# One-token attention over a long cache: value loads issued on ScalarE's queue instead of SyncE's

## The chip, the cores and the metric

The kernel runs on one core of a Trainium2 chip. The metric is the device time of one execution in microseconds (us); the value of the kernel before is the median of two runs. The profile is one execution of the same program, recorded by the hardware profiler; its times are counted from the first instruction of the span.

## The reference

One transformer block for a single token (sequence length 1, width 640) with conditioning. What matters for the time is the attention: 32 heads, each with its own keys and values of 16384 x 128 in bf16.

```python
mod = (_silu(c) @ w_mod)                   # six vectors of 640: sa, ca, ga, sb, cb, gb
h = _layernorm(x) * (1 + ca) + sa
q = h @ wq                                 # 32 heads of 128
scores = einsum('bhqd,bhkd->bhqk', q, k_cache) * 128 ** -0.5
p = softmax(scores)
o = einsum('bhqk,bhkd->bhqd', p, v_cache)
x = x + ga * (o @ wo)
h = _layernorm(x) * (1 + cb) + sb
x = x + gb * ((silu(h @ w_gate) * (h @ w_up)) @ w_down)
```

The keys of a head are 4 MiB (4096 KB in the profile's lists) and so are its values: 256 MiB over 32 heads. All weights together are 22 MB more. Nothing is used twice, so everything goes once from HBM into SBUF.

## The kernel before

**An order written out by hand.** The program is built by a small planner (`_Plan`). Every operation is given an engine, a position (a number that looks like a time in us), the operations that it depends on, and a function that emits it. `emit` sorts the operations of each engine by position; each engine then runs its list strictly in that order, and waits on a semaphore ahead of an operation where a dependency is not already known to be met. A position therefore decides only the order on its engine. `plan.dma` adds a transfer; its engine is `"sp"` (SyncE) unless `eng` says otherwise, and a transfer waits in the list of the engine that issues it like any other operation. All transfers are recorded at L71.

**Heads.** `TK(h)` is 20.0 + 19.8 h, the nominal start of head h. For each head:

- VectorE (DVE) multiplies the keys by the query in place (L420, one instruction over 128 x 16384), adds halves in three folds (L422, L429 twice), reduces to 128 x 128 scores (L432, `o_red[h]`) and takes the maximum of each partition (L435).
- GpSimd (POOL) makes the maximum over partitions (L438); ScalarE (ACT) turns it into a bias (L440) and writes the exponentials (L442, `o_exp[h]`); POOL sums (L445); ACT inverts the sum by logarithm and exponential (L447, L449).
- TensorE (PE) multiplies the exponentials by the values in 32 matmuls (L459, `o_pvlast[h]`). ACT scales the result into SBUF (L465, "acc"), PE folds it (L472), and ACT places it for the output product (L493, L496, or L505 for the last four heads).

**Rings.** `kring` has two slots for keys and `vring`, inside the tile `vbig`, two for values; head h uses slot h % 2. The keys of head h+1 may be loaded once `o_red[h-1]` has read the slot for the last time; the values of head h once `o_pvlast[h-2]` has. The query weights lie over a part of `vring`, so the first two value loads wait for all query products (`o_q_all`). Each load of a head is 128 rows, one per partition, of 32 KB contiguous in HBM. The keys of head 0 come in four parts and the values of head 31 in three (`VSPLIT`).

**Queues before.** SyncE's list is: the conditioning weights, the query weights, the keys of heads 0 and 1, then values 0, keys 2, values 1, keys 3, values 2 and so on, with keys h+1 directly ahead of values h. After keys 31 and values 30 come the output weights `wo` in three transfers (position `TL + 9.0`), the three parts of values 31, and, once `o_red[31]` is done, the feed-forward weights (`w_gate`, `w_up`, and `w_down` in five transfers), which lie over the key slots. ACT issues only the two tiny loads of `c` and `x` at the start.

**End.** After the values of head 31 have been multiplied (L483) come the output product (L541), a layer norm, gate and up (L605), down (L623), a transpose and the store.

Of the kernel before, what the change touches and what calls it, by code (L numbers as in the profile page):

```python
# [141 lines left out]
def build(nc, A_x, A_k, A_v, A_wq, A_wo, B_wg, B_wu, B_wd, c_in, w_mod, out):  # L142
    H, S, Dh = A_k.shape[1], A_k.shape[2], A_k.shape[3]
# [19 lines left out]
    def TK(h):  # L163
        return 20.0 + PERIOD * h

    es = ExitStack()
    with es:
        block = es.enter_context(nc.Block())
        plan = _Plan(nc, es)
# [15 lines left out]
        vring = vbig[:, 0:2 * TT * 128].rearrange("p (s t d) -> p s t d", s=2, t=TT)  # L185
# [126 lines left out]
        def f_mod(e, wv, m0, m1, cols):  # L312
# [11 lines left out]
            deps=[o_mod, o_xn], name="t1")  # L324
# [36 lines left out]
        kv = lambda t, h: t[0, h].rearrange("(p t) d -> p t d", p=128)  # L361
        d_k = [None] * H
        d_v = [None] * H
# [10 lines left out]
        def load_k(h):  # L374
            s2 = h % 2
            deps = [o_red[h - 2]] if h >= 2 else []
            if h == 0:
                KP = TT // NKP0
                d_k[0] = [plan.dma(0.2 + 0.01 * c, kring[:, 0, c * KP:(c + 1) * KP, :], kv(A_k, 0)[:, c * KP:(c + 1) * KP, :],
                                   ("k0", c), name="dma_k0_%d" % c) for c in range(NKP0)]  # L380
                return
            d_k[h] = [plan.dma(TK(h - 1) + 8.8 if h > 1 else 0.3, kring[:, s2], kv(A_k, h), ("k", s2), deps=deps, name="dma_k%d" % h)]

        def load_v(h, pos):
            s2 = h % 2
            cuts = VSPLIT if h == H - 1 else [0, TT]
            deps = [o_pvlast[h - 2]] if h >= 2 else o_q_all
            d_v[h] = [plan.dma(pos + 0.01 * c, vring[:, s2, a:b, :], kv(A_v, h)[:, a:b, :],
                               ("v", s2, c), deps=deps, name="dma_v%d_%d" % (h, c)) for c, (a, b) in enumerate(zip(cuts, cuts[1:]))]

        load_k(0)
        load_k(1)
# [13 lines left out]
        for h in range(H):  # L406
            base = TK(h)
            s2 = h % 2
            if h + 1 < H and h >= 1:
                load_k(h + 1)  # L410
            load_v(h, base + 8.9 + (0.5 if h == H - 1 else 0.0))

            kslot = kring[:, s2]
            npc = len(d_k[h])
# [2 lines left out]
            for c in range(npc):  # L417
# [3 lines left out]
                         deps=[d_k[h][c], o_qbc[h]], name="mult%d_%d" % (h, c))  # L421
                fd.append(op(DVE, base + 3.3 * c + 2.2 + (6.6 if npc == 1 else 0.0), lambda e, ksl=ksl: e.tensor_tensor(  # L422
                    out=ksl[:, :, 0:64], in0=ksl[:, :, 0:64], in1=ksl[:, :, 64:128], op=ALU.add),
                    deps=[o_m], name="fold1_%d_%d" % (h, c)))
            prev = fd
            w = 64
            for i in range(2):
# [3 lines left out]
                    deps=prev, name="fold%d_%d" % (i + 2, h))]  # L431
            o_red[h] = op(DVE, base + 18.2, lambda e, s2=s2, kslot=kslot, w=w: e.tensor_reduce(  # L432
                out=S_sb[:, s2], in_=kslot[:, :, 0:w], axis=AX.X, op=ALU.add),
                deps=prev + [o_exp[h - 2] if h >= 2 else None], name="red%d" % h)
# [9 lines left out]
                deps=[o_nb, o_red[h], o_pvlast[h - 2] if h >= 2 else None], name="exp%d" % h)  # L444
# [8 lines left out]
            if h < H - 1:  # L453


                def f_pv(e, s2=s2):
# [10 lines left out]
                    deps=[o_pvlast[h], o_rl, o_diag[h - 2] if h >= 2 else None], name="acc%d" % h)  # L467
# [21 lines left out]
            if h < HD:  # L489
# [5 lines left out]
                    deps=[done, o_rl], name="on%d" % h)  # L495
                o_z[h] = op(ACT, base + 29.2, lambda e, h=h, g=g, n=n, o=(h - h0) * jw, jw=jw: e.activation(  # L496
                    out=Z[:, g, o:o + jw], in_=msk[n][:], func=ACTF.Copy, scale=on_f[:, h:h + 1]),
                    deps=[o_on[h], o_msk[n]], name="z%d" % h)
                if h == h0 + n - 1:
                    o_am = op(PE, base + 29.4, lambda e, g=g, n=n: e.matmul(A_ps[:, 0:n], lhsT=Z[:, g], rhs=e8[n][:], start=True, stop=True),  # L500
                              deps=[o_z[i] for i in range(h0, h0 + n)] + [o_e8[n], o_as[g - 1] if g else None], name="am%d" % g)
                    o_as[g] = op(ACT, base + 29.6, lambda e, h0=h0, n=n: e.activation(out=A_sb[:, h0:h0 + n], in_=A_ps[:, 0:n], func=ACTF.Copy),
                                 deps=[o_am], name="as%d" % g)
            else:
                o_on[h] = op(ACT, base + 29.0 + (0.7 if h == H - 1 else 0.0), lambda e, h=h, sc=sc: e.activation(  # L505
                    out=On[:, h - HD:h - HD + 1], in_=OT_ps[:, h:h + 1], func=ACTF.Copy, scale=sc),
                    deps=[done, o_rl], name="on%d" % h)
# [4 lines left out]
        a = 0  # L512
        while a < len(GROUPS):
            b = a
            while b < len(GROUPS) and GROUPS[b][1] == GROUPS[a][1]:
                b += 1
            (h0, n), h1 = GROUPS[a], GROUPS[b - 1][0] + GROUPS[b - 1][1]
            d = plan.dma(TO + 0.01 * a, wo_v[:, h0:h1, :].rearrange("p (g k) n -> p g (k n)", k=n),
                         A_wo[h0 * 128:h1 * 128, :].rearrange("(g p k) n -> p g (k n)", p=128, k=n),
                         ("wo", a), deps=[o_mod_b, o_mod], name="dma_wo%d" % a)  # L520
            d_wo += [d] * (b - a)
            a = b
# [4 lines left out]
        for g in list(range(len(GROUPS))) + [None] * (H - HD):  # L527
            if g is not None:
                ks = [k for k, gg in wo_seq if gg == g]
                deps, pos = [o_as[g], d_wo[g]], TL + 29.45 + 0.005 * g  # L530
            else:
                k = HD + len(o_wo) - len(GROUPS)
                ks = [k]
                deps, pos = [o_on[k], d_wo1], TL + (29.48 + 0.001 * (k - HD) if k < H - 1 else 29.8)
# [39 lines left out]
        for a in range(2 * NP2, FCH):  # L574
# [6 lines left out]
                  deps=[o_abf, o_modc], name="ga_attn")  # L581
        o_x1 = op(DVE, TE + 0.2, lambda e: e.scalar_tensor_tensor(
            out=x1[:], in0=tt2[:], scalar=1.0, in1=x_res[:], op0=ALU.mult, op1=ALU.add, accum_out=st[:, 4:5]),
            deps=[o_ga, o_xf], name="x1")
# [3 lines left out]
            deps=[o_xc1, o_rstd1, o_onep_b], name="t2")  # L588
        o_h2 = op(DVE, TE + 1.1, lambda e: e.tensor_tensor(out=h2_col[:], in0=tt3[:], in1=sb_, op=ALU.add),
                  deps=[o_t2], name="h2_col")  # L590
# [26 lines left out]
        for i, (a, b) in enumerate(wd_parts):  # L617
            def f_down(e, a=a, b=b):
                last = None
                for cc in range(KC):  # L620
# [7 lines left out]
                  deps=[prev, o_modc], name="gb_ffn")  # L628
# [10 lines left out]
def bass_adaLN_cond__gqa_block_cached__swiglu_ffn__decode_kernel(  # L639
    nc: bass.Bass,  # L640
    A_x: bass.AP,
    A_k_cache: bass.AP,
    A_v_cache: bass.AP,
    A_wq: bass.AP,
    A_wo: bass.AP,
    B_x: bass.AP,
    B_w_gate: bass.AP,
    B_w_up: bass.AP,
    B_w_down: bass.AP,
    c: bass.AP,  # L650
    w_mod: bass.AP,
    out: bass.AP,
):
    build(nc, A_x, A_k_cache, A_v_cache, A_wq, A_wo, B_w_gate, B_w_up, B_w_down, c, w_mod, out)
# [28 lines left out]
```

## Time and profile before

| | |
|---|---|
| time, median of 2 runs | 689.57 us (689.49 to 689.65) |
| span of the profiled execution | 684.5 us, 4723 instructions |
| the rest of a run's time, outside the span | 5.05 us (689.57 less 684.5) |
| VectorE busy | 617.5 us, 90% of the span |
| TensorE, ScalarE, GpSimd busy | 351.0, 79.6 and 360.0 us |
| moved by DMA | 290.79 MB, mean 425 GB/s |
| share of the transfers' packets on SyncE's queue (q1) | 13668 packets, 290.48 MB |
| on ScalarE's queue (q10) | 288 packets, under 0.01 MB |

The profile gives its execution no time other than its span, so sums are made against the 684.5 us, and 5.05 us are added to come to the time of a run. Busy time is not the measure here: two resources, VectorE and the 16 DMA engines, are both close to full over nearly the whole span, and the question is which of them waits for the other, and when.

### The profile page before, as it was taken

What the parts mean: (1) busy time and instruction counts of PE and PEld (TensorE: products, weight loads), DVE (VectorE), ACT (ScalarE), POOL (GpSimd) and SP (SyncE); (2) the same over time, 40 slices, a digit from 0 to 9 for tenths busy, and PEclk for the clock granted to TensorE, in tenths of its full rate; (3) what the DMA queues carried; (4) which work ended last, traced back from release to release, by engine and by line L of the source; (5) the groups of instructions that cost most, each with busy time, mean ns of one, the idle gap of its engine ahead of it and who ended that gap; (6) DMA issues with size and microseconds to landing.
All of it is one profiled execution on the core that took longest, in us unless ns stands there. A gap on an engine that the chain in (4) does not pass through costs nothing.

```text
span 684.5 us, 4723 instructions
## 1 busy us (share of the span) xinstructions
PE 351.0 (51%) x1941; PEld 150.8 (22%) x1942; DVE 617.5 (90%) x226; ACT 79.6 (12%) x281; POOL 360.0 (53%) x71
## 2 busy tenths in 40 slices
PE   0545344656554454655554444565544545655464
PEld 0322111222221121222221121222211212222154
DVE  0299999999999999999999999999999999999911
ACT  0111011011101111011101111011101110111010
POOL 0005765655567765655567766655533644555400
PEclk9976677676677667677777767767776677677765
DMA  8999999999999999999999999999999999999997
GB/s 369 417 438 432 431 429 437 429 433 433 429 434 431 431 429 430 433 431 434 433 431 429 433 429 431 430 431 433 432 433 433 429 432 429 435 433 428 413 413 277
DMA packets 13979, 290.79 MB, mean 425 GB/s; under 512 B 1605, under 2 KB 2309, under 8 KB 4485
## 3 DMA queue, kind: packets, MB, share of 16 engines
q1 hardware_dynamic: 13668, 290.48, 99.1%
q8 instruction: 15, 0.25, 0.1%
q10 hardware_dynamic: 288, 0.00, 0.0%
q14 instruction: 8, 0.06, 0.0%
HBM read 290.48 MB, written 0.00 MB: 424 GB/s over the span
## 4 chain that ended last, share of the span: by engine, by line
DVE 79%; DMA 18%; SPq 2%; issue 1%; PE 0%; ACT 0%; DVEq 0%
DVE kring L420 35%; DVE kring L422 18%; DVE kring L429 14%; DMA kring<-in_A_k_cache_dram 12%; DVE S_sb L432 9%; DMA vbig<-in_A_wq_dram 4%; SPq L71 2%; DMA kring<-in_B_w_down_dram 2%; DVE pm L435 1%; PE psb L339 0%; PE psb L623 0%; ACT qbc L343 0%; DVE e L402 0%; DVE msk L397 0%; PE psb L631 0%
## 5 line engine op out<-in xcount | busy, mean ns | idle before, releaser
L459 PE MATMUL psb<-vbig,P_sb 128*4 128x512 bf16 x992 | 284.4, 458 | 268.1 <-ACT P_sb L442 193.9
L438 POOL PARTITION_ALL_REDUCE gm<-pm x32 | 229.2, 7163 | 239.9 <-DVE pm L435 239.9
L420 DVE TENSOR_TENSOR kring<-kring,qbc 128x16384 bf16<-128x16384 bf16 (+1 forms) x35 | 278.4, 7953 | 5.9 <-ACT qbc L343 4.6
L459 PEld LDWEIGHTS psb<-vbig,P_sb 128*4 128x4 bf16 x992 | 94.8, 98 | 444.6 <-ACT P_sb L442 219.9
L445 POOL PARTITION_ALL_REDUCE Ls<-rs x32 | 129.7, 4054 | 34.2 <-ACT P_sb L442 34.2
L422 DVE TENSOR_TENSOR kring<-kring 128x8192 bf16<-128x8192 bf16 (+1 forms) x35 | 142.1, 4059 | 1.2
L429 DVE TENSOR_TENSOR kring<-kring 128x4096 bf16<-128x4096 bf16 x64 | 112.5, 1758 | 2.2
L432 DVE TENSOR_REDUCE S_sb<-kring 128x128 f32<-128x2048 bf16 x32 | 73.2, 2286 | 1.1
L472 PE MATMUL psb<-ident_f,acc_sb 4*128 4x1 f32 x248 | 32.5, 248 | 23.8 <-ACT acc_sb L465 23.8
L465 ACT ACTIVATE acc_sb<-psb,rl 4x512 f32<-4x512 f32 x31 | 21.0, 677 | 176.2 <-PE psb L459 176.2
L472 PEld LDWEIGHTS psb<-ident_f,acc_sb 4*128 4x128 f32 x248 | 29.8, 186 | 39.5 <-ACT acc_sb L465 39.5
L440 ACT ACTIVATE nb<-gm 128x1 f32<-128x1 f32 x32 | 6.4, 201 | 193.6 <-POOL gm L438 193.6
L447 ACT ACTIVATE lnl<-Ls 128x1 f32<-128x1 f32 x32 | 6.5, 203 | 133.7 <-POOL Ls L445 133.7
L580 DVE TENSOR_TENSOR tt<-attn_bf,modb 128x5 f32<-128x5 bf16 x1 | 0.2, 166 | 14.5 <-ACT attn_bf L579 14.5
L442 ACT ACTIVATE P_sb<-S_sb,nb 128x128 bf16<-128x128 f32 x32 | 12.9, 402 | 1.2
L289 PE MATMUL psb<-st,ones_f 128*128 128x1 f32 x4 | 1.2, 363 | 22.8 <-ACT x_f L306 22.1
L339 PE MATMUL psb<-vbig,h_col 128*128 128x512 bf16 x39 | 10.8, 448 | 2.4 <-DMA vbig<-in_A_wq_dram 2.4
L291 DVE SCALAR_TENSOR_TENSOR xc<-x_f,psb 128x5 f32<-128x5 f32 x1 | 0.2, 161 | 12.2 <-PE psb L289 12.2
L435 DVE TENSOR_REDUCE pm<-S_sb 128x1 f32<-128x128 f32 x32 | 9.2, 286 | 1.1
L496 ACT ACTIVATE Z<-msk,on_f 128x16 bf16<-128x16 f32 (+1 forms) x28 | 8.7, 310 | 0.9
L493 ACT ACTIVATE on_f<-psb 128x1 f32<-128x1 f32 x28 | 4.8, 171 | 31.9 <-PE psb L472 30.7
L283 DVE TENSOR_SCALAR dd<-ec 128x5 f32<-128x5 f32 x1 | 0.2, 172 | 8.9 <-ACT ec L282 8.9
(72 smaller groups left out, 78.3 us busy)
## 6 DMA issues: line engine op xcount, KB each, us to landing
kring<-in_A_k_cache_dram SPq DMA_DIRECT2D x31, 4096.0 KB, 18.4
vbig<-in_A_v_cache_dram SPq DMA_DIRECT2D x31, 4096.0 KB, 27.6
vbig<-in_A_wq_dram SPq DMA_DIRECT2D x1, 5120.0 KB, 26.5
wreg<-in_w_mod_dram SPq DMA_DIRECT2D x1, 4800.0 KB, 14.6
kring<-in_A_k_cache_dram SPq DMA_DIRECT2D x4, 1024.0 KB, 31.4
wreg<-in_A_wo_dram SPq DMA_DIRECT2D x1, 3840.0 KB, 38.0
kring<-in_B_w_gate_dram SPq DMA_DIRECT2D x1, 2160.0 KB, 18.9
kring<-in_B_w_up_dram SPq DMA_DIRECT2D x1, 2160.0 KB, 23.8
```

What stands on the lines that cost most here:

```text
L71: return e.dma_start(out_ap, in_ap)
L420: o_m = op(DVE, base + 3.3 * c, lambda e, ksl=ksl, qb=qb: e.tensor_tensor(out=ksl, in0=ksl, in1=qb, op=ALU.mult), deps=[d_k[h][c], o_qbc[h ...
L422: fd.append(op(DVE, base + 3.3 * c + 2.2 + (6.6 if npc == 1 else 0.0), lambda e, ksl=ksl: e.tensor_tensor(out=ksl[:, :, 0:64], in0=ksl[:, ...
L429: prev = [op(DVE, base + 15.5 + 1.5 * i, lambda e, kslot=kslot, w=w: e.tensor_tensor(out=kslot[:, :, 0:w], in0=kslot[:, :, 0:w], in1=kslot ...
L432: o_red[h] = op(DVE, base + 18.2, lambda e, s2=s2, kslot=kslot, w=w: e.tensor_reduce(out=S_sb[:, s2], in_=kslot[:, :, 0:w], axis=AX.X, op= ...
L435: o_max = op(DVE, base + 18.5, lambda e, h=h, s2=s2: e.tensor_reduce(out=pm[:, h:h + 1], in_=S_sb[:, s2], axis=AX.X, op=ALU.max), deps=[o_ ...
L438: o_gm = op(POOL, base + 19.0, lambda e, h=h: e.partition_all_reduce(gm[:, h:h + 1], pm[:, h:h + 1], channels=128, reduce_op=bass.bass_isa ...
L442: o_exp[h] = op(ACT, base + 19.4, lambda e, h=h, s2=s2: e.activation(out=P_sb[:, s2], in_=S_sb[:, s2], func=ACTF.Exp, scale=SCALE, bias=nb ...
L445: o_L = op(POOL, base + 20.0, lambda e, h=h: e.partition_all_reduce(Ls[:, h:h + 1], rs[:, h:h + 1], channels=128, reduce_op=bass.bass_isa. ...
L459: last = e.matmul(acc_ps[s2][0:4, :], lhsT=P_sb[:, s2, 4 * c:4 * c + 4], rhs=vring[:, s2, 4 * c:4 * c + 4, :].rearrange("p t d -> p (t d)" ...
L465: o_acc[h] = op(ACT, base + 28.6, lambda e, h=h, s2=s2: e.activation(out=acc_sb[:, s2], in_=acc_ps[s2][0:4, :], func=ACTF.Copy, scale=rl[0 ...
L472: last = e.matmul(OT_ps[:, h:h + 1], lhsT=acc_sb[:, s2, 128 * i:128 * (i + 1)], rhs=ident_f[:, i:i + 1], start=(i == 0), stop=(i == 3))
```

## The change

The values are issued from ScalarE's list (`eng="act"`), and their position moves from 8.9 after the start of head h to 28.65 after the start of head h-2. That is the place right behind the scaling at L465 ("acc", 28.6) of head h-2, ahead of that head's L493 and L496 and of L440 of head h-1. Values 0 and 1 stand at 4.75 and 4.85, behind the last copies of the query stage on ACT (L356, L394). The dependencies are as before. Keys and all weights stay on SyncE, in the same order, without the values between them.

```diff
@@ load_v(h, pos)
             s2 = h % 2
             cuts = VSPLIT if h == H - 1 else [0, TT]
             deps = [o_pvlast[h - 2]] if h >= 2 else o_q_all
-            d_v[h] = [plan.dma(pos + 0.01 * c, vring[:, s2, a:b, :], kv(A_v, h)[:, a:b, :],
-                               ("v", s2, c), deps=deps, name="dma_v%d_%d" % (h, c)) for c, (a, b) in enumerate(zip(cuts, cuts[1:]))]
+            d_v[h] = [plan.dma(pos + 0.01 * c, vring[:, s2, a:b, :], kv(A_v, h)[:, a:b, :], ("v", s2, c), deps=deps,
+                               name="dma_v%d_%d" % (h, c), eng="act") for c, (a, b) in enumerate(zip(cuts, cuts[1:]))]
@@ for h in range(H)
             if h + 1 < H and h >= 1:
                 load_k(h + 1)
-            load_v(h, base + 8.9 + (0.5 if h == H - 1 else 0.0))
+            load_v(h, TK(h - 2) + 28.65 if h >= 2 else 4.75 + 0.1 * h)
```

The lists of PE, DVE and POOL do not change. SyncE's list loses 34 transfers, ScalarE's gains 34.

## The prediction

> **What bounds the kernel now.** I read the page first: the busy shares, the slices, then the lists of waits, and last the timeline of one ordinary head and of the end.
>
> ```profile
> span 684.5 us, 4723 instructions
> ...
> DVE  0299999999999999999999999999999999999911
> ...
> GB/s 369 417 438 432 431 429 437 429 433 433 429 434 431 431 429 430 433 431 434 433 431 429 433 429 431 430 431 433 432 433 433 429 432 429 435 433 428 413 413 277
> ```
>
> VectorE is full from the second slice to the last two, and the transfers run at 429 to 435 GB/s all the while. At 431 GB/s a load of 4096 KB (4.194 MB) takes 9.73 us of all 16 engines, so keys and values of one head take 19.46 us. VectorE needs 19.28 us for a head, from the next view (109.74 to 129.02). The two are equal to 1%, and the slower is the transfer side.
>
> ```profile
> 109.38 0.68 ACT L465 ACTIVATE acc_sb<-psb,rl 4x512 f32<-4x512 f32 x1 [5.07 <-PE psb L459]
> 109.53 0.33 SPq L71 DMA_DIRECT2D kring<-in_A_k_cache_dram  x1
> 109.74 8.68 DVE L420 TENSOR_TENSOR kring<-kring,qbc 128x16384 bf16<-128x16384 bf16 x1
> 109.90 0.43 SPq L71 DMA_DIRECT2D vbig<-in_A_v_cache_dram  x1
> 109.92 8.72 POOL L438 PARTITION_ALL_REDUCE gm<-pm  x1 [6.07 <-DVE pm L435]
> ...
> 128.81 0.33 SPq L71 DMA_DIRECT2D kring<-in_A_k_cache_dram  x1
> 129.02 8.68 DVE L420 TENSOR_TENSOR kring<-kring,qbc 128x16384 bf16<-128x16384 bf16 x1
> ```
>
> Keys h+1 are issued as soon as L432 of head h-1 has left the slot, and are needed 19.49 us later (109.53 to 129.02). The list of issues says when they come:
>
> ```profile
> kring<-in_A_k_cache_dram SPq DMA_DIRECT2D x31, 4096.0 KB, 18.4
> vbig<-in_A_v_cache_dram SPq DMA_DIRECT2D x31, 4096.0 KB, 27.6
> ...
> c_col<-in_c_dram ACTq DMA_DIRECT2D x1, 1.2 KB, 8.9
> x_col<-in_A_x_dram ACTq DMA_DIRECT2D x1, 1.2 KB, 20.5
> ```
>
> 18.4 us, of which 9.73 are their own and 8.7 the rest of the values queued ahead. So the margin of the keys is 1.1 us in the median, and it is used up late in the run: the list of waits and the chain that ended last show the first, small waits for keys from 495 us on.
>
> ```profile
> DVE kring L420 <- DMA kring<-in_A_k_cache_dram: 1.2, 4, 0.5
> ```
> ```profile
> 495.28 20.34 DMA kring<-in_A_k_cache_dram
> 515.62 0.02 issue
> 515.64 8.70 DVE kring L420
> ```
>
> The run ends on the transfers: the last group of down weights lands at 680.55 in the chain (666.96 + 13.59), 4.0 us ahead of the end at 684.5. The end can only come earlier if the engines move the same bytes faster.
>
> **The change, part by part.**
>
> *Issues off SyncE.* 34 issues of 0.33 to 0.43 us leave a sequencer that waits 563.6 us for L435/L432 in any case; keys are issued 0.02 us after L432 ends, now as then (107.22 + 2.29 = 109.51, issue 109.53). Worth nothing. If that wait were gone, it would be 0.4 us a head.
>
> *Issues onto ScalarE.* 32 heads, 34 issues, 0.40 to 0.45 us by the two ACT issues at the start, some 14 us on a queue busy 79.6 us. Behind them stand L493, L496 and L440 of the next head. L440 waits for POOL in 27 heads, 193.6 us in all, 7 us each, which hides 0.43. In heads where VectorE was kept waiting, POOL's maximum is done in 0.35 us (495.67) and not 8.72, and then 0.43 us shows in L442; but L459 then starts up to 7 us early, so nothing is late. Cost 0.
>
> *When values are issued.* Values h follow L465 of head h-2: 109.38 + 0.68 = 110.1 in place of 109.90 here; in other heads within 1 us either way. Values 0 go from 39.10 to about 41.9 (behind L394), values 1 from 51.11 to 42.3. By 4.7 us SyncE has issued 18.5 MB, good for 42.9 us from 2.15, so the engines stay covered to 45 us. Cost 0.
>
> *Two queues in place of one, which is what decides.* Before, keys h+1 stood ahead of values h in one line. Now each engine has keys in one ring and values in another. What it does then is shown by the loads of `c` and `x`: 288 packets of ACT's queue, 18 an engine, needed until 1.21 + 20.5 = 21.7 us beside the weights' rows of 37.5 KB, 1.42 us each. From 2.15 us on that is 1.09 us a turn: about one row between two small packets, so the queues take turns. Keys and values have rows of one size (32 KB, 9.73 / 8 = 1.22 us), so they share half and half.
>
> Three things follow. First, no byte moves faster: the windows 5 to 10, 10 to 15 and 15 to 20 us, where both queues were busy, hold 415, 437 and 410 GB/s, no better than the loop. Second, sharing alone gives keys 8 + 8 rows, 19.46 us in place of 18.4. Third, what stood ahead in line hid the start of a transfer, and no longer does. I take the start from the first window:
>
> ```profile
> 0.00:5.00 5.00, 0.00 (x0) 0.00 (x0) 0.18 (x2) 1.28 (x1) 0.39 (x5) 1.00 0.65 246
> ```
>
> 246 GB/s over 5 us are 1.23 MB, 2.85 us at 431; so packets ran from 2.15 us, 1.36 us after the first issue at 0.79.
>
> Follow two heads, with keys h+1 issued at t. Their packets are there at t + 1.36, the last engine has up to one row of values to finish (1.22), then 8 rows of keys with 7 of values between take 18.25: landed at t + 20.83. VectorE was ready at t + 19.49 and waits 1.3. Keys h+2 are issued at t + 0.21 + 19.07 = t + 19.28, their packets are there as the former end, so no start shows: t + 20.83 + 19.46 = t + 40.29, where VectorE is ready at t + 40.11; it waits 0.2. The third issue is at t + 20.83 + 19.07 = t + 39.90. So two heads take 39.90 if values are always queued. They are not: at that pace the engines have 39.90 - 38.92 = 0.98 us to spare, so now and then the ring of values is empty and keys run alone. The other bound is engines that never rest: 38.92. I take three quarters of the way, 39.65 or 19.82 a head, since values come in whole loads and are empty for only a part of the keys' time.
>
> VectorE's last L432 then ends at 50.74 + 31 x 19.82 = 665 in place of 651.5. Much of this does not reach the end, because at 651.5 the engines still had 13.5 us of older work (values 31 landed at 665.2, where L483 could finish). What is left is summed from the landing of keys 31, 19.1 us ahead of that L432: output weights 5.24 MB, 12.2 us; values 31, 9.7; the rest of values 30, 1. That is 22.9, so 3.8 us remain when the feed-forward weights join. These are 6480 KB, 16.1 us at the 413 GB/s of the last full slices; add 1.3 for engines that end unevenly (the window 675 to 680 holds 308 GB/s) and 4.0 from the last landing to the end. Span: 665 + 3.8 + 16.1 + 1.3 + 4.0 = 690.2; with 5.05 outside it 695.2. I take **695 us**, 0.8% more. The same sum at 38.92 for two heads ends on the engines' work as before, 689.6; at 39.90 the last L432 ends at 50.74 + 31 x 19.95 = 669.2, the span is 694.4, the time 699.4.
>
> How long a start takes on a busy ring is not in the trace. Below, the store at the end was issued and landed in 1.2 us (0.31 and a wait of 0.9), near the 1.36. Above, I allow twice 1.36: two heads take 41.26 if values are always queued, three quarters of the way again is 40.67, the last L432 ends at 681 and the time is 711. I keep 1.36, which was measured on a load, and both ends for the range.
>
> The Trainium skill ("DMA: Bandwidth & Descriptors", "Issuing engines are not separate DMA queues") speaks against a gain: queues of several issuers end on the same 16 engines, interleave, and save only issue time. The trace agrees where both queues ran, in the 410 to 437 GB/s above. The same page ("Latency and other measured facts") puts the first byte of a load issued on these queues near 0.6 us, where the first window gives 1.36; by its figure two heads would take at most 39.1 us and the time would be about 690.
>
> **Rivals.**
>
> *The engines stay full, so nothing changes.* For it: total work is the same, the end is bound by transfers, and values 31 are no longer held up on SyncE, where three issues took 14.59 us (from 631.76) behind the output weights. That saved wait moves no byte sooner, as older work filled the engines; I give it 1 us at most. Against: one load of keys at a time in its ring must leave gaps. Time 689, or 688.5.
>
> *Slower by over 2%.* Place: the start of each load of keys. If an engine finishes two rows of values it has already fetched before it turns to the new ring, or if the start is twice as long, every second head waits 1.3 + 1.2 = 2.5 us. Two heads take at most 41.1, three quarters of the way 40.56; the last L432 ends at 679.4, the span is 679.4 + 25.2 = 704.6, the time **710**. It decides from 20.08 us a head, where the last L432 ends at 673. Against it: the turns of `c` and `x`, one for one.
>
> *Faster.* It would need over 431 GB/s. Even at the 435 of the best full slice of the loop, 290.5 MB take 668 us against 674: 6 us, under 1%.
>
> **How the numbers follow.** Between 690 and 700, as summed: 0.50. Engines stay full, 688 to 690: 0.17. Slower, 703.4 and more: 0.27. The ground between 700 and 703.4: 0.05. Faster by over 2%: 0.01. A change of 2% (13.8 us) is about what a measurement of this kernel tells from none. Within 2% is 0.50 + 0.17 + 0.05 = 0.72. The range of 689 to 709 leaves out some 0.07 below and 0.13 above.
>
> **What would show it.** Right: VectorE's wait for keys goes from 1.2 us in all to some 15, mostly in every second head; issue to landing of keys goes from 18.4 to about 20.3, of values falls from 27.6 to about 21 to 25; ACT's queue has half the bytes; slices of the loop fall to about 425 GB/s; the last L432 ends near 665 and the tail behind it shrinks from 33 to 25 us. Wrong: waits for keys in every head by 1 us or more, or none; slices of the loop under 420 GB/s with a full DMA row, which would mean that turns between the rings cost something; or values so late that L459 delays the next issue.

## The result and the profile after

The changed kernel takes **722.67 us** (721.61 and 723.74) against 689.57: 4.8% slower, ratio 1.048, 95% interval 1.0461 to 1.0498. The prediction was 695 with a range of 689 to 709. The sign was right, the size was not.

Lines of the page of the changed kernel, then of its list of waits and its list of issues (KB each, us from issue to landing):

```profile
span 719.9 us, 4723 instructions
...
DVE  0099799989989998998899899899988999999861
...
GB/s 376 417 411 429 428 432 319 433 437 433 433 427 426 433 241 435 433 432 427 428 437 264 409 437 437 434 430 428 284 426 428 432 432 434 386 340 416 419 383 271
```
```profile
DVE kring L420 <- DMA kring<-in_A_k_cache_dram: 39.2, 20, 3.9
```
```profile
kring<-in_A_k_cache_dram SPq DMA_DIRECT2D x31, 4096.0 KB, 22.6
vbig<-in_A_v_cache_dram ACTq DMA_DIRECT2D x31, 4096.0 KB, 23.2
```

VectorE now waits for keys in 20 of 31 heads, 39.2 us in all (1.2 before). Keys land 22.6 us after their issue (18.4), values 23.2 (27.6): what values gained, keys lost, and keys are what is needed first. And something new: most slices still run at 426 to 437 GB/s, as before, but five are down to 241 to 340. Each of these five holds a stretch in which all 16 engines had nothing to move.

The 35.4 us that the span grew (684.5 to 719.9) add up in two ways. On VectorE: the first L432 ends 4.8 us later (55.55 for 50.72), the 31 heads after it take 20.64 us in place of 19.38, 39.1 us together, and the tail behind the last L432 shrinks from 33.0 to 24.4. On the DMA engines, from the trace's records of single packets (a few overlap, so idle and busy do not add up exactly to the span): a mean engine is idle 38.4 us against 7.8, and its packets take 684.3 us against 679.7. These are two views of one loss, not two losses.

Two words below: a *slot* is a place in SBUF for the keys or the values of one head, and a *ring*, as in the prediction, is what one queue has waiting on one DMA engine.

One of the holes, first in the windows of 3 us (the last column is GB/s), then in the timeline:

```profile
253.00:256.00 3.00, 2.71 (x7) 0.85 (x8) 3.00 (x1) 0.24 (x2) 2.67 (x1) 0.50 0.94 404
256.00:259.00 3.00, 3.00 (x11) 0.92 (x9) 2.97 (x2) 0.41 (x2) 0.97 (x1) 0.62 0.05 22
259.00:262.00 3.00, 3.00 (x16) 1.17 (x15) 2.93 (x3) 0.00 (x0) 0.00 (x0) 1.00 0.00 0
262.00:265.00 3.00, 1.85 (x12) 1.13 (x10) 2.96 (x3) 0.99 (x3) 1.95 (x1) 1.00 0.59 175
```
```profile
223.53 0.35 POOL L438 PARTITION_ALL_REDUCE gm<-pm  x1 [20.90 <-DVE pm L435]
...
224.29 8.69 DVE L420 TENSOR_TENSOR kring<-kring,qbc 128x16384 bf16<-128x16384 bf16 x1 [0.85 <-DMA kring<-in_A_k_cache_dram]
...
233.81 0.33 ACTq L71 DMA_DIRECT2D vbig<-in_A_v_cache_dram  x1
...
243.58 8.68 DVE L420 TENSOR_TENSOR kring<-kring,qbc 128x16384 bf16<-128x16384 bf16 x1
243.76 8.72 POOL L438 PARTITION_ALL_REDUCE gm<-pm  x1 [10.54 <-DVE pm L435]
...
252.75 0.40 ACT L442 ACTIVATE P_sb<-S_sb,nb 128x128 bf16<-128x128 f32 x1
253.29 9.51 PE L459 MATMUL psb<-vbig,P_sb 128*4 128x512 bf16 x32 [17.73 <-ACT P_sb L442]
260.35 2.29 DVE L432 TENSOR_REDUCE S_sb<-kring 128x128 f32<-128x2048 bf16 x1
...
262.85 0.33 ACTq L71 DMA_DIRECT2D vbig<-in_A_v_cache_dram  x1
```

Values are issued at 233.81 and next at 262.85, 29 us apart. The cause can be followed upwards in the trace. Where VectorE had been kept waiting for keys, GpSimd's maximum takes 0.35 us (223.53), so the exponentials, L459 and the release of a value slot come early. In the next head the keys are in time, VectorE goes straight on with L420, and the maximum beside it takes 8.72 us (243.76). Now everything behind it comes late, and the ring of values is empty by then; keys run alone, land at 258, and their next slot is free only when L432 ends at 262.64. Between the keys issued at 243.37 and those at 262.66 no load is issued, and from 257.9 to 263.6 no engine has a packet. The other holes look alike: in all five the two issues of values are 27.8 to 32.7 us apart (23.4 at most elsewhere), and GpSimd's maximum takes 8.7 to 8.9 us in just ten heads, two in a row at each hole, and 0.35 in the other 22. In the profile of before there is no such hole in the loop: values stood behind keys in the line, and some 8.7 us of them were left when the next keys were issued.

### The profile page after: what moved, and what is told of

The parts are those of the page before. It is cut to its first block, busy times and chain, and to the rows that moved or that the text cites. A ratio compares the mean times of both kernels' runs of the same rounds, so it can differ in the third digit from the quotient of the medians.

```text
span 719.9 us, 4723 instructions
## 1 busy us (share of the span) xinstructions
PE 341.0 (47%) x1941; PEld 149.2 (21%) x1942; DVE 618.7 (86%) x226; ACT 79.6 (11%) x281; POOL 203.9 (28%) x71
## 4 chain that ended last, share of the span: by engine, by line
DVE 56%; DMA 41%; PE 1%; issue 1%; ACT 0%; ACTq 0%; DVEq 0%
DMA kring<-in_A_k_cache_dram 35%; DVE kring L420 25%; DVE kring L422 13%; DVE kring L429 10%; DVE S_sb L432 7%; DMA x_col<-in_A_x_dram 4%; DMA kring<-in_B_w_up_dram 2%; DVE pm L435 0%; PE psb L623 0%; PE psb L605 0%; PE psb L317 0%; PE psb L339 0%; ACT qbc L343 0%; PE psb L289 0%; PE psb L296 0%
## 5 line engine op out<-in xcount | busy, mean ns | idle before, releaser
L459 PE MATMUL psb<-vbig,P_sb 128*4 128x512 bf16 x992 | 274.0, 445 | 302.8 <-ACT P_sb L442 259.4
L420 DVE TENSOR_TENSOR kring<-kring,qbc 128x16384 bf16<-128x16384 bf16 (+1 forms) x35 | 278.5, 7957 | 42.4 <-DMA kring<-in_A_k_cache_dram 39.2
L438 POOL PARTITION_ALL_REDUCE gm<-pm x32 | 95.0, 2969 | 441.8 <-DVE pm L435 421.8
L459 PEld LDWEIGHTS psb<-vbig,P_sb 128*4 128x4 bf16 x992 | 92.5, 95 | 471.3 <-ACT P_sb L442 278.7
L422 DVE TENSOR_TENSOR kring<-kring 128x8192 bf16<-128x8192 bf16 (+1 forms) x35 | 142.1, 4059 | 1.2
L445 POOL PARTITION_ALL_REDUCE Ls<-rs x32 | 107.8, 3369 | 32.2 <-ACT P_sb L442 32.2
L432 DVE TENSOR_REDUCE S_sb<-kring 128x128 f32<-128x2048 bf16 x32 | 73.1, 2286 | 1.1
L465 ACT ACTIVATE acc_sb<-psb,rl 4x512 f32<-4x512 f32 x31 | 21.0, 678 | 162.7 <-PE psb L459 162.5
L440 ACT ACTIVATE nb<-gm 128x1 f32<-128x1 f32 x32 | 6.4, 201 | 266.6 <-POOL gm L438 266.6
L289 PE MATMUL psb<-st,ones_f 128*128 128x1 f32 x4 | 1.2, 363 | 29.1 <-ACT x_f L306 28.4
L496 ACT ACTIVATE Z<-msk,on_f 128x16 bf16<-128x16 f32 (+1 forms) x28 | 8.7, 310 | 0.9
L541 PE MATMUL psb<-A_sb,wreg 128*128 128x1 bf16 x140 | 3.9, 165 | 9.3 <-DMA wreg<-in_A_wo_dram 9.3
L493 ACT ACTIVATE on_f<-psb 128x1 f32<-128x1 f32 x28 | 4.8, 171 | 31.9 <-PE psb L472 30.7
## 6 DMA issues: line engine op xcount, KB each, us to landing
kring<-in_A_k_cache_dram SPq DMA_DIRECT2D x31, 4096.0 KB, 22.6
vbig<-in_A_v_cache_dram ACTq DMA_DIRECT2D x31, 4096.0 KB, 23.2
```

Source lines behind the costliest of these rows:

```text
L420: o_m = op(DVE, base + 3.3 * c, lambda e, ksl=ksl, qb=qb: e.tensor_tensor(out=ksl, in0=ksl, in1=qb, op=ALU.mult), deps=[d_k[h][c], o_qbc[h ...
L438: o_gm = op(POOL, base + 19.0, lambda e, h=h: e.partition_all_reduce(gm[:, h:h + 1], pm[:, h:h + 1], channels=128, reduce_op=bass.bass_isa ...
L445: o_L = op(POOL, base + 20.0, lambda e, h=h: e.partition_all_reduce(Ls[:, h:h + 1], rs[:, h:h + 1], channels=128, reduce_op=bass.bass_isa. ...
L459: last = e.matmul(acc_ps[s2][0:4, :], lhsT=P_sb[:, s2, 4 * c:4 * c + 4], rhs=vring[:, s2, 4 * c:4 * c + 4, :].rearrange("p t d -> p (t d)" ...
L465: o_acc[h] = op(ACT, base + 28.6, lambda e, h=h, s2=s2: e.activation(out=acc_sb[:, s2], in_=acc_ps[s2][0:4, :], func=ACTF.Copy, scale=rl[0 ...
```

## The experiments

Three explanations were held against each other. **Keys late:** a new load starts late on a busy engine and then shares it, so keys, which VectorE needs within 19.5 us, land after 22. **Two queues as such:** ScalarE's issues or switches between rings cost engine time. **The start of the kernel**, 4.8 us, as `x` landed at 28.0 us in place of 21.7. Each ratio is against the kernel before on the same chip; that one took 686.1 to 686.5 us, 689.9 or 690.1 on the chips used here, so runs are best compared by their ratios. Where the expectations speak of a start of 3.8 and 1.3 us, they mean the time from the issue of a load of keys to its first row; under "Shorter rows of values" it is given in two ways.

**The loads of c and x first on SyncE**, in the changed kernel and in the one before.

```diff
-d_c = plan.dma(0.0, c_col[:], ..., name="dma_c", eng="act")
-d_x = plan.dma(0.01, x_col[:], ..., name="dma_x", eng="act")
+d_c = plan.dma(-0.02, c_col[:], ..., name="dma_c")
+d_x = plan.dma(-0.01, x_col[:], ..., name="dma_x")
```

> The changed kernel with the two tiny loads of c and x issued first on SyncE, ahead of the weights, so that they take no turns with the weights' rows. In the profile of the changed kernel x landed at 28.0 us against 21.7 before, and the last reduction of head 0 ended 4.8 us later. If this belongs to the change: time 717 to 719, the first L432 ends near 46 to 50 us. If it does not reach the end: 722.

> The kernel before with the same edit to c and x. The end is bound by the transfers there, so an earlier start of VectorE should be worth little: 689 to 690, at most 1 us faster. If the early start counts in full: 684 to 686.

Measured: 720.7 us for the changed kernel so edited, ratio 1.0506 (1.047 to 1.0542), no better than 1.048 without; 686.86 for the one before, ratio 1.0007 (0.9993 to 1.0022). The first L432 ended at about 51.5 us in both. The late start is not the cause. It isn't the change's either: `x` was late in some kernels and early in others here (22.2 us in the next run; 28 in one of the runs below that has all large loads on SyncE). In the kernels looked at, `x` was early where ACT's packets were the first on the engines, and late where SyncE's were.

**The new positions alone**, values back on SyncE.

```diff
-    name="dma_v%d_%d" % (h, c), eng="act") for c, ...
+    name="dma_v%d_%d" % (h, c)) for c, ...
```

> The new positions alone: values stay on SyncE, but at the new place, which is ahead of keys h+1 and behind keys h in SyncE's list. One line, no turns. If the queue is what costs, keys start behind no held rows but behind the 9.7 us of values: they land about 20.8 us after the issue, wait for keys at each head 1 us or so, time 700 to 715. If the place in the order is all that costs: 722.

Measured: 720.05 us, ratio 1.0491 (1.0471 to 1.0511), as slow as the change. The issues:

```profile
kring<-in_A_k_cache_dram SPq DMA_DIRECT2D x31, 4096.0 KB, 21.9
vbig<-in_A_v_cache_dram SPq DMA_DIRECT2D x31, 4096.0 KB, 17.9
```
```profile
DVE kring L420 <- DMA kring<-in_A_k_cache_dram: 37.6, 14, 5.6
```

There is one queue here and nobody takes turns, but values stand ahead of keys, keys land at 21.9, VectorE waits 37.6 us and the engines idle 34.6. (In 14 heads the wait for a value slot also holds up the issue of keys behind it in SyncE's list, by 1.1 us at most.) So a second queue is not needed for the loss: it is enough that keys no longer come first. The expectation of 700 to 715 for this order was too low: it had VectorE wait some 1 us a head, and a head took 1.26 us longer (20.64 for 19.38).

**Shorter rows of values.** If rings take turns row by row, halving the rows of values gives keys two thirds of an engine while both are busy, quartering them four fifths.

```diff
-cuts = VSPLIT if h == H - 1 else [0, TT]
+cuts = VSPLIT if h == H - 1 else [TT * i // 2 for i in range(3)]      # 16 KB; 4 and 5 for 8 KB
-o_pvlast[h] = op(PE, base + 28.0, f_pv, deps=[o_exp[h], d_v[h][0], ...
+o_pvlast[h] = op(PE, base + 28.0, f_pv, deps=[o_exp[h]] + d_v[h] + [...
```

> Values in two transfers of 16 KB rows on ScalarE's queue, keys in 32 KB rows. Theory 1: start 1.3 + 2 x 0.61 = 2.5 us, keys get two thirds of the engine, land about 18 us after the issue, time 692 to 702. If what an engine holds is a time or a number of bytes and not a number of rows, the start stays at 3.8 and the time at 705 to 715. Rival 1: over 715.

> Values in four transfers of 8 KB rows on ScalarE's queue, keys as they are (32 KB rows). In the changed kernel the first row of keys starts 3.8 us after the issue when the other ring is busy and 1.3 us when it is idle. Theory 1 (an engine has already taken two rows of the busy ring, and rings take turns row by row): the start falls to 1.3 + 2 x 0.31 = 1.9 us, keys get four fifths of the engine, land some 15 to 16 us after the issue, VectorE's wait for keys falls from 39 us to under 5, and the time to 690 to 697. Rival 1 (what costs is two rings that fall into step and run dry together, whatever the rows): start about 3.8, time over 715. Rival 2 (issues on ScalarE's sequencer cost): four times as many issues, time over 725.

Measured: 693.95 us with 16 KB, ratio 1.0055 (1.004 to 1.007); 702.86 with 8 KB, ratio 1.0182 (1.0167 to 1.0198). Keys land at 18.8 and 16.3 us, and VectorE waits for them 2.3 us in all with 16 KB and not at all with 8 KB. From the run with 16 KB:

```profile
kring<-in_A_k_cache_dram SPq DMA_DIRECT2D x31, 4096.0 KB, 18.8
```
```profile
DVE kring L420 <- DMA kring<-in_A_k_cache_dram: 2.3, 6, 0.5
```

And from the run with 8 KB:

```profile
kring<-in_A_k_cache_dram SPq DMA_DIRECT2D x31, 4096.0 KB, 16.3
```
```profile
PE psb L459 <- DMA vbig<-in_A_v_cache_dram: 258.4, 27, 16.9
```

The larger share for keys is confirmed. The rest of the expectation is not. The run with 8 KB missed its 690 to 697: now values come last, TensorE waits for them, and they land at 681.2 us (665.2 in the kernel before); the tail behind the last L432 grows from 33.0 to 46.8 us. The run with 16 KB fell into its range, but not for the reason given, as the start of keys did not shrink with the rows. From the packets' records, the first rows of a load of keys start this long after the beginning of its issue (medians over the loads):

```
                    first of the 16 engines    mean of the 16 engines
rows of 32 KB, values in the ring (28 loads)    3.5 us    4.2 us
               ring of values empty (2 loads)   1.0       1.2
rows of 16 KB (30)                              3.4       3.8
rows of  8 KB (30)                              3.4       3.6
```

By the expectations, an engine that held two rows would have given 2.5 us with 16 KB and 1.9 with 8 KB. So work from the other ring adds some 2.5 us to the first start (3.5 for 1.0), and not a number of rows. Whether that is a time or a number of bytes, and why, these runs don't say. The mean is above the first by about half a row of values (0.65, 0.35, 0.2 us). The records don't name the engine, but packets that follow each other without a gap can be put together. The rows of one engine so found, in order of time (K keys, v values), with rows of 32 KB from 322 to 352 us and, in the run with 8 KB, from 200 to 222:

```
vKvvvKvKvKvKKvKvKvKvvvKv
vKvKvKKvKvvvvvvvvvvvvvvvvvvvvvvvvKvKvKvKvK
```

With few exceptions one row from each ring in turn, whatever its length; between two loads of keys there are values only. The Trainium skill ("DMA: Bandwidth & Descriptors", "Queues, rings and completion order") has an engine go round its rings packet by packet, a typical packet being about 9 to 17 descriptors. The runs agree on the turns, but a turn here is one row.

**The mirror: shorter rows of keys.** As many bytes, short rows and issues as in the run with 16 KB values, but now values are favoured.

```diff
-d_k[h] = [plan.dma(..., kring[:, s2], kv(A_k, h), ("k", s2), ...)]
+d_k[h] = [plan.dma(... + 0.01 * c, kring[:, s2, c * KQ:(c + 1) * KQ, :], kv(A_k, h)[:, c * KQ:(c + 1) * KQ, :], ("k", s2, c), ...) for c in range(2)]     # KQ = TT // 2
```

L420 then waits for both halves.

> Mirror of the run with values in 16 KB rows: now keys come in two transfers of 16 KB rows, values keep rows of 32 KB, queues and positions as in the changed kernel. The bytes, the number of short rows and of issues are the same as in that run (693.95 us), only the share is turned round: keys get one third while values are in the ring. If what matters is which of the two the engines favour: keys land 23 to 24 us after the issue, VectorE waits for them 39 us or more, time 722 to 737. If short rows or more, smaller transfers are what helped there: 694 to 705.

Measured: **773.02 us**, ratio 1.1278 (1.1243 to 1.1314), 36 us more than expected at most.

```profile
DVE kring L422 <- DMA kring<-in_A_k_cache_dram: 90.0, 15, 13.9
```

(L422 is L420 here, two lines moved.) Keys land up to 34 us after the issue, and the engines idle 78.5 us. This run and its mirror have the same bytes, the same number of short rows and the same number of issues (the added ones are on SyncE here, on ScalarE there), and their ratios are 1.1278 and 1.0055. So neither short rows nor the number of issues is behind the loss; which of the two streams the engines favour is.

**Short rows for both, on two queues and on one.** Keys and values each in four transfers of 8 KB rows.

> Keys and values both in four transfers of 8 KB rows, keys on SyncE, values on ScalarE: equal shares as in the changed kernel, but short rows. This tells the start from the share. Theory 1: start 1.9 us, keys land at 1.9 + 19.5 + 0.3 = 21.7 us against 22.6, wait for keys about half, 15 to 20 us, time about 700 to 706. If the share alone counts: 720. If the start alone counts: 693.

> Control: the kernel before, one line on SyncE, with keys and values in 8 KB rows and four transfers each. All theories: rows of 8 KB cost nothing by themselves, time within 3 us of the kernel before (689 to 693); if it is slower by more, the three runs with short rows have to be read against this one.

Measured: 729.7 us on two queues, ratio 1.0603 (1.055 to 1.0655); 702.08 on one, ratio 1.0172 (1.0157 to 1.0187). Both expectations missed. Rows of 8 KB do cost: they take 314 ns each, 8 KB at 26.1 GB/s an engine, where rows of 32 KB take 1218 ns, 26.9 GB/s; the engines' work rises from 679.7 to 700.9 us on one queue. Against its control, the run on two queues, where shares are equal, loses 27.6 us: shorter rows alone do not help, an unequal share does.

**Control with 16 KB values on one queue.**

> Control for the run with values in 16 KB rows: the kernel before, one line on SyncE, values in two transfers of 16 KB rows. The engines' own work rose by 4.8 us with these rows on two queues (684.5 against 679.7 us a DMA engine). If that is the rows: time 3 to 5 us over the kernel before, and the two queues with 16 KB values cost nothing beyond their rows. If it is the two queues: no change here.

Measured: 688.61 us against 686.5, ratio 1.0032 (1.0018 to 1.0047). The rows explain about half of the 1.0055 of the two-queue run; two queues with keys favoured cost some 0.2% beyond that, and the two intervals overlap.

**Values later on ScalarE's queue**, with rows of 32 KB: first behind the exponentials of the head before, then behind L420 of their own head.

```diff
-load_v(h, TK(h - 2) + 28.65 if h >= 2 else 4.75 + 0.1 * h)
+load_v(h, TK(h - 1) + 19.45 if h >= 1 else 4.75)                # behind the exponentials
```
```diff
+if h >= 2: load_v(h, base + 0.01, [o_m])                        # behind L420: o_m added to deps
```

> As the changed kernel, but values of head h stand on ScalarE's list right behind the exponentials of head h-1 (L442), about 10 us after the keys of head h+1 are issued, in place of behind L465 of head h-2, when both are issued together. Rows stay at 32 KB. Theory 1 with the issue times: the start of keys stays at 3.8 us where values are in the ring, but only some 4 to 6 us of values are left, so keys land about 16 us after the issue; wait for keys under 6 us, time 690 to 697. If the loss lies in taking turns or in the queue itself whatever the times of issue: over 715.

> Rows of 32 KB, values on ScalarE's queue, but values of head h wait in addition for the product at L420 of head h, that is until 8.9 us after the keys of head h+1 were issued, whatever GpSimd does. (Behind the exponentials, as in the run before, this distance shrank whenever VectorE had been kept waiting, as GpSimd's maximum is then done early; VectorE waited 18.2 us there and the time was 697 to 706.) Theory: keys first is what counts; they find at most some 6 us of values in the ring, land 16 to 18 us after the issue, wait for keys under 6 us, engines idle some 10 us, time 690 to 698 with a spread of a few us at most. If two lines lose time in any order: 702 or more again.

Measured: 702.79 us (697.48 to 705.88), ratio 1.0232 (1.0184 to 1.028), for the first: better by half, not to 690 to 697, with 18.2 us of waits for keys left. The exponentials are no firm mark, as they end 1.4 to 3.5 us after L432 in heads in which keys were late, and 9.8 us after it in most others. For the second: **694.73** (694.56 to 695.48), ratio 1.0124 (1.011 to 1.0139). In its list of waits (L421 is L420):

```profile
DVE kring L421 <- DMA kring<-in_A_k_cache_dram: 3.7, 4, 2.9
```

39.2 us of waits have become 3.7, with two queues, full rows and as many issues as in the change. No hole of over 2 us is left in the loop. Keys land 19.8 us after the issue, later than the 16 to 18 expected, but in time. This is the change with three quarters of its loss taken out (ratio 1.0124 for 1.048), by the order alone.

**The output weights too.** In that run they landed at 671.8 us (654.8 in the kernel before), and the end waited for them. That their rows of 10 KB and less get a small share beside values would follow from the shares above; the run moves them out of that.

```diff
-plan.dma(TO + 0.01 * a, wo_v[...], ..., name="dma_wo%d" % a)
+plan.dma(TK(H - 2) + 0.02 + 0.01 * a, wo_v[...], ..., name="dma_wo%d" % a, eng="act")     # all three loads
```

> The run with values behind the product at L420 (694.73 us, 8.2 over the kernel before on the same chip), with the three loads of the output weights moved to ScalarE's queue, right behind values 30 and so ahead of values 31 in that line, as in the kernel before. In the run without this the output weights, in rows of 10 KB and less beside rows of 32 KB, landed at 671.8 us, and L541, L483 and everything behind waited for them. Theory: with keys first and the output weights out of the unequal sharing, two queues are worth the same as one: 686 to 690 us against 686.5, that is within 0.5%. If two queues cost by themselves: 693 or more. If two queues have a gain to give that the order had hidden: under 684.

Measured: 694.54 us, ratio 1.006 (1.0047 to 1.0074), on a chip where the kernel before took 689.89: half of the remaining loss is gone, and by its ratio it ends between the two expectations, which were made for 686.5. Much of what is left stands at the start in its profile:

```profile
GB/s 372 415 396 434 424 333 415 427 430 437 426 430 431 437 430 429 433 433 429 432 428 437 429 428 432 434 430 428 433 431 432 430 431 430 435 430 429 415 416 247
```

The sixth slice lacks about 97 of 430 GB/s over 17.3 us, 3.9 us of work, and 4.1 us is what the run is over by its ratio (0.6% of 689.89). It falls behind values 0 and 1, which are still issued together ahead of keys 2. That it would go with them was not tried. No run was faster than the kernel before.

## Why the prediction was wrong, step by step

**Right.** What bounds the kernel; the free issues (the runs with 16 KB values and behind L420 have as many on ScalarE or more, and end at 1.0055 and 1.0124); turns of one row and equal shares; that VectorE would wait for keys; the tail, 25.2 us from the last L432 forecast, 24.4 measured; that nothing moves faster.

**The step that failed is the sum for two heads.** Its upper bound was 39.90 us, taken as the price "if values are always queued", and measured were 41.3 (2 x 20.64). Two terms were wrong.

1. *The start.* 1.36 us came from the first window, on idle engines, and it is about right there: 1.0 us for the first engine and 1.2 in the mean where the ring of values was empty. With the one row of values that may be under way the text had 1.36 + 1.22 = 2.58 us; on busy engines it is 4.2 in the mean. The text noted that no row shows this, and allowed twice 1.36 as a bound, 3.94 with the row and 711 us; that is a little too small as well. Put 4.2 into the same lines: keys land at t + 4.2 + 18.25 = t + 22.4, in place of 20.83, beside the 22.6 of the list. So sharing alone, 18.25 us, costs keys no more than standing in line did (18.4); what they lost is the start.
2. *The spare time.* The text held that values running dry give time back, as keys then run alone, and took three quarters of the way for it. Keys do run alone, and land early (18.5, 14.9, 15.0, 16.1 and 16.1 us after the issue ahead of the five holes). But with both slots of keys and both of values full or in use, no load can be issued until VectorE or TensorE frees one, and the engines idle. The five holes are 28.4 us. Time that the engines lose is not given back in a kernel that they bound. The sum had no term for this, although "L459 delays the next issue" stood, for late values, among the signs of being wrong. What sets it off was in the profile of before: GpSimd's 8.72 us beside L420 against 0.35, noted in the text as "nothing is late", moves the exponentials, and with them the release of values, by 8.4 us from head to head (9.8 us after L432 for 1.4).

How much each is worth is an estimate, by the prediction's own sum. With 4.2 in place of 2.58, two heads take at most 41.5, three quarters of the way is 40.9, and the time comes to some 714 us: 19 of the missing 28 us. The measured 41.3 is over nine tenths of the way, which is 6 or 7 us more. The rest is the start of the kernel, 4.8 us later, against 0.8 in the tail and the next term.

A small term was off as well: 5.05 us were added for what lies outside the span. In the run of the changed kernel that was profiled it was 1.7 us (721.61 less 719.9), and 1.7 to 1.9 in the other runs of which both figures are on record. So about 3.3 of the 5.05 us were a difference between two executions of the kernel before. And one line was read a little low: the best slice of the loop before holds 437 GB/s, not 435; nothing followed from it.

The rival that was given 0.27 is the nearer one, in part by luck: its place (the start of each load of keys) and its size there (2.5 us in every second head; measured 2.0 a wait in 20 heads) were right. Of its two mechanisms, two rows held was refuted by the short rows; a start twice as long was nearer, but still short. Its price of 710 lacks the holes. The forecast and the rival "engines stay full" both rested on engines that find work whenever a ring is free. The range, 709 at the top, held only that.

The rule from the Trainium skill ("DMA: Bandwidth & Descriptors") that more issuing queues only save issue time ("Issuing engines are not separate DMA queues") pointed the right way, but it tells only that there is no gain. The 0.6 us for the first byte from the same page ("Latency and other measured facts") agrees with idle engines here if it is counted from the end of the issue: the first row then starts 0.64 us later. With work in the other ring it is 3.2 us by the same count.

## What to carry to other kernels

In this kernel the one queue was also a schedule: two streams share saturated DMA engines and have two slots each, the line says which of them is served first, and the one that is needed soonest must be ahead (ratio 1.0491 with values ahead of keys in one line, 1.0124 with keys ahead on two queues). Before streams are split over queues, ask what each load's deadline is, and when the next slot of each stream comes free; if both fall at the same time, sharing can make the urgent load late and leave the engines without work afterwards, as it did here. If they have to be split, put the order back by a dependency on something that comes at a fixed distance, or give the urgent stream the longer rows (ratio 1.0055).

## What the runs showed of the hardware that was not expected

- A load of keys issued while the 16 engines work for the other ring starts, on the first of them, 3.5 us after its issue, and 1.0 us after it when they are idle; rows of 8, 16 or 32 KB in the other ring make next to no difference (3.4, 3.4, 3.5).
- The share of a ring follows the length of its rows: halving the rows of keys or of values moved the ratio from 1.048 to 1.128 or to 1.0055.
- Rows of 8 KB run at 26.1 GB/s an engine, rows of 32 KB at 26.9; over 268 MB that was 1.7% of the time on one queue.
- GpSimd's maximum over partitions (L438) took 0.35 us at 223.53, when VectorE was idle, and 8.72 us at 243.76, when VectorE was in the product at L420 (243.58 to 252.26), that is until the product had ended.
